# Attention and a gelu layer in parallel: dense groups on one PSUM bank of their own, with half a unit between groups

## The chip, the cores and the metric

The kernel runs on one core of a Trainium2 chip. The metric is the device time of one execution in microseconds (us). Of the kernel before, three runs gave 1554.35, 1555.06 and 1557.26 us, with a median of 1555.06 us. One further execution was profiled; its own time is 1555.34 us, of which the profile's span covers 1553.6 us.

The engines are TensorE (PE, with its weight loads as PEld), VectorE (DVE), ScalarE (ACT), GpSimd (POOL) and SyncE (SP), which issues the DMAs.

## What is computed

The input is normalized (layer norm over 512 columns), and two branches read it: attention with 32 heads of 16 columns over 2048 rows, and a two-layer net of width 1792 with gelu (tanh form). The result is the sum of the input and both branches.

```
xn = _layernorm(x, axis=-1)
return x + _A_ref(xn, A_wqkv, A_wo) + _B_ref(xn, B_w1, B_b1, B_w2, B_b2)

# _A_ref: scores = q @ k.T * (Dh ** -0.5);  p = softmax(scores);  (p @ v) @ wo
# _B_ref: h = gelu(x @ w1 + b1);  h @ w2 + b2
```

## The kernel before

**Units and halves.** Attention is cut into 32 tiles (8 groups of 4 heads, 4 blocks of 512 queries) of 16 units each, 512 units in all. A unit has two halves, and in each of them `unit` writes the same kinds of products into TensorE's queue, in this order:

- two score products for the row maximum (`s_half`, tile `pS`), two score products for the exponential (`e_half`, tile `pT`), each as four 32-column pieces;
- four weighted sums (`v_half`, tile `pV`, fp32, two passes each, so eight instructions in the trace), on 64 of the array's 128 rows;
- dense products (`dense`, tile `pD`, fp16) on the other 64 rows, four 32-column pieces each. The halves change sides: the first half of a unit has its dense products on rows 0 to 63, the second on rows 64 to 127.

VectorE takes the row maximum from `pS` (L259), ScalarE turns `pT` into `pe` with an exponential (L304). The order of instructions on every engine is the order in which the program writes them. Through a counter, the first weighted sum and the first dense product of a half wait for the last ones of the half before (`enter`, `leave`), because both sides add into the same banks.

**Dense work.** All matrix products outside attention are cut into groups (`Group`), of which one is open at a time: 24 projections for later heads (12 products for each side of the array), 56 hidden groups `hidden_group` (12 products a side), 32 sum groups `sum_group` (21 a side), and at the end the output projection. `dense` adds up to `pace` products of the open group to a half. For the projections the pace is `FAST`, four in every half; for hidden and sum groups it is `MEAN`, three in each half of one unit and four in each of the next. When both sides of a group are done, `ended` closes it, and ScalarE empties its bank: `pf` (L506) of a projection, `hh` (L1005) of a hidden group, `yt` (L1031) of a sum group. That instruction stands in ScalarE's queue ahead of the exponentials of the next half.

After `hh`, gelu goes three steps on GpSimd, then ScalarE's tanh (L972, two units after those steps have been written), then four steps on GpSimd, after which the piece counts as done for the sum groups (`ready`, `usable`).

**Banks.** PSUM has eight: three for `pS`, three for `pT`, one for `pD` and one for `pV`. `banks` takes the next of a kind in turn. `hold` (for the dense groups, L409 to L413) takes a bank out: the first group takes the one of kind D, and when it ends, that bank joins the end of T's list; the next group takes the bank at the head of T's list. So a bank goes round between scores and dense groups.

Of the kernel before, what the change touches and what calls it, by code (L numbers as in the profile page):

```python
# [19 lines left out]
D = 512  # L20
# [8 lines left out]
NG = H // 4  # L29
VW = DH + 1  # L30
LEAD = 20
FAST, MEAN, SLOW, LATE = (4, 4), (3, 4), (3, 3), (6, 6)
MEASURE = (3, 0, 1, 2)
HALF = 1300
POOL_NS = 2500
# [12 lines left out]
def layer_kernel(ctx: ExitStack, tc: tile.TileContext, x, wqkv, wo, w1, b1, w2, b2, out):  # L48
# [55 lines left out]
    def bank_tile(k, tag):  # L104
        return ps.tile([P, QB], F32, tag=f"B{k}", bufs=1, name="p" + tag)

    def banks(tag):
        k = free_banks[tag].pop(0)
        free_banks[tag].append(k)
        return bank_tile(k, tag)  # L110

    def hold(tag, other):
        k = free_banks[tag if free_banks[tag] else other].pop(0)
        return bank_tile(k, tag), k
# [39 lines left out]
    PAIRS = ((0, 0), (0, 1), (1, 0))  # L154
# [4 lines left out]
    def given(engine, ns):  # L159
        backlog[engine] += ns  # L160
# [52 lines left out]
    def later(n, fn, local=False):  # L213
        queue.append((slot[0] + n, fn, local))
# [10 lines left out]
    def pooled(*todo):  # L225
        steps.extend(todo)
# [169 lines left out]
    NU = NG * NQB * 16  # L396
# [10 lines left out]
    def dbank():  # L407
        turn[0] += 1
        if pos[0] < LEAD:  # L409
            return banks("T"), None  # L410
        if pos[0] > NU:
            return banks("S"), None
        return hold("D", "T")  # L413

    class Group:

# [122 lines left out]
        for _ in gen:  # L539
            pass  # L540

    pos, spent, cur = [0], [False], [None]
    feed, xbs, wcs = [], {}, {}

    def fetch_x(b):
        if b < NQB:
            xbs[b] = feed[0].tile([P, 2, NC, QB], F16, name="xb", bufs=1)
            for c in range(NC):
                later(1 + c, lambda c=c: nc.sync.dma_start(xbs[b][:, :, c], xn_d[:, :, c, b * QB:(b + 1) * QB]))

    def fetch_w1(n):
        if n < NQB * NF:
            wcs[n] = feed[0].tile([P, 2, NC, P], F16, name="wc", bufs=3)
            nc.sync.dma_start(wcs[n], w1_d[n % NF // 2, :, n % 2])

    def group(gen):

        if cur[0] is None and not spent[0]:
            cur[0] = next(gen, 0)
            if cur[0] == 0:  # L560
                cur[0], spent[0] = None, True
        return cur[0]

    def ended():

        if cur[0] is not None and cur[0].over():
            done, cur[0] = cur[0], None
            done.end()

    def burst(gen, n):  # L570

        while n > 0 and (f := group(gen)) is not None:
            if not f.usable():
                break
            f.product(2)
            n -= 1
            ended()

    def dense(gen, side):

        f = group(gen)
        for _ in range(0 if f is None else (f.pace if pos[0] <= NU + 1 else LATE)[pos[0] % 2]):
            if not f.usable(side):
                return
            f.product(side)
# [376 lines left out]
    def mlp():  # L962
        m2 = st2p
        w2_s = m2.tile([P, 2, NF, D], F16, name="w2_s")
        b2_b = m2.tile([P, D], F32, name="b2_b")
        done = set()

        def gelu(hh, g, b, f):
            t1 = m2.tile([P, QB], F32, name="t1", bufs=2)

            def tanh():
                nc.scalar.activation(t1, t1, AF.Tanh, scale=GELU_C * GELU_A)  # L972
                given("act", 600)
                later(1, rest, True)

            def rest():
                pooled((690, lambda: nc.gpsimd.tensor_scalar(t1, t1, 1.0, gs[:, 1:2], op0=ALU.add, op1=ALU.mult)),  # L977
                       (1280, lambda: nc.gpsimd.tensor_tensor(t1, t1, hh, op=ALU.mult)),  # L978
                       (620, lambda: nc.gpsimd.tensor_scalar(g[:, 0, f, :], t1, 1.0, 0.0, op0=ALU.mult, op1=ALU.add)),
                       (1160, lambda: nc.gpsimd.tensor_tensor(g[:, 1, f, :], t1, g[:, 0, f, :], op=ALU.subtract)),  # L980
                       (0, lambda: done.add((b, f))))

            pooled((1040, lambda: nc.gpsimd.tensor_tensor(t1, hh, hh, op=ALU.mult)),  # L983
                   (620, lambda: nc.gpsimd.tensor_scalar(t1, t1, 1.0, 1.0 / GELU_A, op0=ALU.mult, op1=ALU.add)),
                   (1280, lambda: nc.gpsimd.tensor_tensor(t1, t1, hh, op=ALU.mult)),  # L985
                   (0, lambda: later(2, tanh, True)))


        HF = NF // 2
        gts, xas = {}, {}  # L990
        for k in range(NF):
            later(3 * k + 2, lambda k=k: nc.sync.dma_start(w2_s[:, :, k], w2_d[:, :, k]))
        later(12, lambda: nc.sync.dma_start(b2_b, b2[None, :].to_broadcast([P, D])))

        def hidden_group(s, f):
            b, k = s // 2, s % 2 * HF + f
            if f == 0:
                gts[s] = m2.tile([P, 2, HF, QB], F16, name="g", bufs=2)
            g, xb, wc = gts[s], xbs[b], wcs[b * NF + k]
            later(1, lambda: fetch_w1(b * NF + k + 2))  # L1000

            def hidden(hp):
                hh = m2.tile([P, QB], F32, name="hh", bufs=3)
                scale, bias = fac1[0][:, k // 2:k // 2 + 1], b1_s[:, k:k + 1]
                nc.scalar.activation(hh, hp, AF.Identity, bias=bias, scale=scale)  # L1005
                given("act", 700)
                later(1, lambda: gelu(hh, g, s, f), True)

            return Group([lambda c=c, i=i, j=j: (wc[:, i, c, :], xb[:, j, c, :]) for c in range(NC) for i, j in PAIRS],
                         dbank, hidden, pace=MEAN)  # L1010

        def sum_group(s, q):
            b, t, g = s // 2, s // 2 * 4 + q, gts[s]
            if s % 2 == 0:
                xas[t] = m2.tile([P, D], F32, name="xa", bufs=4)
                nc.sync.dma_start(xas[t], x[t * P:(t + 1) * P, :])
                later(3, lambda: pooled((1280, lambda: nc.gpsimd.tensor_tensor(xas[t], xas[t], b2_b, op=ALU.add))), True)
            xa = xas[t]
            if q == 3 and s % 2 == 0:
                fetch_x(b + 1)  # L1020
            if s == 2 * NQB - 1 and q == 1:

                ocs[2] = feed[0].tile([P, 2, NC, QB], F16, name="xb", bufs=1)
                when((NG - 2) * NQB + 2, lambda: read_o(ocs[2], 2, True), 2)
                for k in range(3):
                    acs[8 + k] = feed[0].tile([P, D], F32, name="ac", tag="wc", bufs=3)
                    later(3 + k, lambda k=k: read_acc(acs[8 + k], 8 + k))

            def store(yp):
                yt = m2.tile([P, D], F32, name="yt", bufs=2)  # L1030
                nc.scalar.activation(yt, yp, AF.Copy, scale=gs[:, 2:3])  # L1031
                given("act", 600)
                add = lambda: nc.gpsimd.tensor_tensor(xa, xa, yt, op=ALU.add)  # L1033
                put = lambda: nc.sync.dma_start(acc_d[t * P:(t + 1) * P, :], xa)
                later(1, lambda: pooled((1280, add), (0, lambda: later(4, put, True) if s % 2 else None)), True)

            return Group([lambda f=f, i=i, j=j: (g[:, i, f, q * P:(q + 1) * P], w2_s[:, j, s % 2 * HF + f, :])
                          for f in range(HF) for i, j in PAIRS], dbank, store, lambda n: (s, n // 3) in done, pace=MEAN)

        for f in range(HF):  # L1040
            yield hidden_group(0, f)
        for s in range(1, 2 * NQB + 1):
            for q in range(4):
                yield sum_group(s - 1, q)
                if s < 2 * NQB and q < 3:
                    for f in range(*((0, 3), (3, 5), (5, 7))[q]):
                        yield hidden_group(s, f)

    def when(t, fn, n=1):

        def step():
            if t in ready and (pos[0] >= NU or pos[0] % 16 in range(4, 14)):
                fn()
            else:
                later(1, step)

        later(n, step)
# [3 lines left out]
    def read_o(oc, qb, early):  # L1061
        for c in range(NC):
            n = 64 if early and c == NC - 1 else P
            nc.sync.dma_start(oc[:n, :, c, :], ot_d[c * P:c * P + n, :, qb * QB:(qb + 1) * QB])  # L1064

    def read_acc(ac, t):
        nc.sync.dma_start(ac, acc_d[t * P:(t + 1) * P, :])
# [123 lines left out]
```

## Time and profile before

| what | value |
|---|---|
| median of three runs | 1555.06 us |
| the profiled execution: its time, its span | 1555.34 us, 1553.6 us |
| TensorE busy | 1514.5 us (97%) |
| VectorE busy | 1401.0 us (90%) |
| ScalarE busy | 1251.6 us (81%) |
| GpSimd busy | 674.6 us (43%) |
| weighted sums (`pV`) | 8192 instructions, 8 per half |
| exponentials, row maxima | 2048 each, 598 and 684 ns in the mean |
| `hh`, tanh, `yt`, `pf` | 56 of 778 ns, 56 of 631 ns, 32 of 689 ns, 21 of 599 ns |

Times inside the trace are counted from the start of the span. Starts are what to read on TensorE: instructions of different rows and columns of the array overlap, and their ends are modelled. The time from the first `pV` of a half to the first `pV` of the next is called the length of the half here. In a table by windows, the number in brackets behind a busy time is the number of instructions that start in the window, up to one at its edge; 8 of `pV` are one half, and 4 of `pD` are one dense product.

### The profile page before, as it was taken

What the parts mean: (1) busy time and instruction counts of PE and PEld (TensorE: products, weight loads), DVE (VectorE), ACT (ScalarE), POOL (GpSimd) and SP (SyncE); (2) the same over time, 40 slices, a digit from 0 to 9 for tenths busy, and PEclk for the clock granted to TensorE, in tenths of its full rate; (3) what the DMA queues carried; (4) which work ended last, traced back from release to release, by engine and by line L of the source; (5) the groups of instructions that cost most, each with busy time, mean ns of one, the idle gap of its engine ahead of it and who ended that gap; (6) DMA issues with size and microseconds to landing.
All of it is one profiled execution on the core that took longest, in us unless ns stands there. A gap on an engine that the chain in (4) does not pass through costs nothing.

```text
span 1553.6 us, 86338 instructions
## 1 busy us (share of the span) xinstructions
PE 1514.5 (97%) x39203; PEld 806.0 (52%) x39203; DVE 1401.0 (90%) x2372; ACT 1251.6 (81%) x2326; POOL 674.6 (43%) x694
## 2 busy tenths in 40 slices
PE   8998999999999999999999999999999999999997
PEld 4434545555555555555555555555555555555443
DVE  7898989999999999999999999999999999999612
ACT  4316878889888888888888888888888888888771
POOL 3113697546465444435443443555254454521000
PEclk9999999999999999999999999999999999999997
DMA  6454576542111311121112111121112111022412
GB/s 210 124 158 142 167 231 197 180 120 88 50 35 47 91 33 34 36 75 42 35 56 65 46 35 35 35 80 55 36 42 60 45 35 35 22 66 60 150 50 86
DMA packets 113671, 123.72 MB, mean 80 GB/s; under 512 B 24988, under 2 KB 85276, under 8 KB 113304
## 3 DMA queue, kind: packets, MB, share of 16 engines
q1 hardware_dynamic: 113304, 118.21, 25.4%
q8 instruction: 306, 5.01, 1.4%
q14 instruction: 61, 0.50, 0.1%
HBM read 80.61 MB, written 37.34 MB: 76 GB/s over the span
## 4 chain that ended last, share of the span: by engine, by line
PE 84%; DVE 8%; ACT 2%; issue 2%; DMA 2%; SPq 1%; POOL 0%; ACTq 0%; POOLq 0%
PE pV L169 25%; PE pS L169 19%; PE pD L169 19%; PE pT L169 17%; DVE mt L259 6%; PE pT L439 1%; PE pS L439 1%; ACT pe L304 1%; ACT t L972 1%; DVE amx L667 1%; PE pT L532 1%; PE pD L439 1%; DMA ac<-acc_d 0%; PE pV L532 0%; SPq L1064 0%
## 5 line engine op out<-in xcount | busy, mean ns | idle before, releaser
L259 DVE TENSOR_REDUCE mt<-pS 128x1 f32<-128x512 f32 x2048 | 1299.9, 684 | 60.7 <-PE pS L169 43.1
L304 ACT ACTIVATE pe<-pT 128x512 f32<-128x512 f32 x2048 | 1100.0, 598 | 169.5 <-PE pS L169 72.3
L169 PE MATMUL pV<-pe,vv 64*32 64x512 f32 x8192 | 1077.6, 595 | 0.2
L169 PE MATMUL pT<-qst,kst 64*32 64x512 f16 x8192 | 708.2, 378 | 10.4 <-ACT pe L304 8.9
L169 PE MATMUL pS<-kst,qst 62*32 62x512 f16 x8192 | 636.8, 378 | 9.3 <-DVE mt L259 6.0
L169 PEld LDWEIGHTS <-qst 62*32 62x32 f16 x8192 | 271.1, 92 | 226.8 <-issue 77.9
L169 PEld LDWEIGHTS <-kst 64*32 64x32 f16 x8192 | 270.2, 91 | 213.7 <-issue 109.5
L169 PE MATMUL pD<-xb,wc 64*32 64x512 f16 x5376 | 370.5, 377 | 0.0
L169 PE MATMUL pD<-w_s,g 64*32 64x512 f16 x5376 | 359.4, 377 | 0.0
L169 PEld LDWEIGHTS pV<-pe,vv 64*32 64x32 f32 x8192 | 181.5, 105 | 111.2 <-PE pV L169 18.0
L983 POOL TENSOR_TENSOR t<-hh 128x512 f32<-128x512 f32 x56 | 58.3, 1042 | 341.2 <-ACT hh L1005 341.2
L169 PEld LDWEIGHTS <-g 64*32 64x32 f16 x5376 | 113.8, 92 | 38.6
L169 PE MATMUL pD<-xt,wqk_h 64*32 64x512 f16 x1920 | 127.6, 377 | 3.5 <-issue 3.5
L169 PEld LDWEIGHTS <-wc 64*32 64x32 f16 x5376 | 112.6, 91 | 31.1
L360 POOL TENSOR_TENSOR osb<-osb,rb 128x512 f32<-128x512 f32 x31 | 39.9, 1287 | 128.1 <-DMA rb<-den_d 95.1
L1033 POOL TENSOR_TENSOR xa<-xa,yt 128x512 f32<-128x512 f32 x32 | 41.0, 1280 | 119.0 <-ACT yt L1031 119.0
L1070 DVE SCALAR_TENSOR_TENSOR ac<-pS,gs,ac 128x512 f32<-128x512 f32 x20 | 15.0, 751 | 67.0 <-PE pT L169 46.9
L978 POOL TENSOR_TENSOR t<-t,hh 128x512 f32<-128x512 f32 x56 | 71.8, 1283 | 4.7
L985 POOL TENSOR_TENSOR t<-t,hh 128x512 f32<-128x512 f32 x56 | 71.7, 1280 | 4.7
L980 POOL TENSOR_TENSOR g<-t,g 128x512 f16<-128x512 f32 x56 | 65.3, 1166 | 4.7
L977 POOL TENSOR_SCALAR t<-t,gs 128x512 f32<-128x512 f32 x56 | 38.8, 693 | 55.5 <-ACT t L972 55.5
L169 PE MATMUL pS<-wo_s,oc 64*32 64x512 f16 x1008 | 61.7, 378 | 0.3
(139 smaller groups left out, 881.1 us busy)
## 6 DMA issues: line engine op xcount, KB each, us to landing
wch<-in_B_w_dram SPq DMA_DIRECT2D x28, 512.0 KB
wc<-w_d SPq DMA_DIRECT2D x56, 256.0 KB
qk_d<-stg SPq DMA_DIRECT2D x32, 256.0 KB
rb<-den_d SPq DMA_DIRECT2D x124, 64.0 KB
w_d<-wsp SPq DMA_DIRECT2D x28, 256.0 KB
kst<-qk_d SPq DMA_DIRECT2D x128, 48.0 KB
qst<-qk_d SPq DMA_DIRECT2D x128, 48.0 KB
xs<-in_A_x_dram SPq DMA_DIRECT2D x16, 256.0 KB
```

Of the source, the lines that this page charges most:

```text
L169: p = nc.tensor.matmul(*args, **kw)
L259: nc.vector.reduce_max(mt_of[t][:, n, qt, kb:kb + 1], s, axis=AX.X)
L304: nc.scalar.activation(pe, st, AF.Exp, scale=exp_scale(g // 2))
L360: pooled((1280, lambda: nc.gpsimd.tensor_tensor(osb, osb, rb, op=ALU.mult)), (620, lambda: nc.gpsimd.tensor_scalar(ot[:, 0], osb, 1.0, 0.0 ...
L439: nc.tensor.matmul(self.bank, lhs, rhs, start=start, stop=self.last and self.over())
L532: nc.tensor.matmul(pj, xt[:, i, c, t * P:(t + 1) * P], wh[j][:, c, :], start=(n == 0), stop=(n == 11))
L977: pooled((690, lambda: nc.gpsimd.tensor_scalar(t1, t1, 1.0, gs[:, 1:2], op0=ALU.add, op1=ALU.mult)), (1280, lambda: nc.gpsimd.tensor_tenso ...
L978: (1280, lambda: nc.gpsimd.tensor_tensor(t1, t1, hh, op=ALU.mult)),
L980: (1160, lambda: nc.gpsimd.tensor_tensor(g[:, 1, f, :], t1, g[:, 0, f, :], op=ALU.subtract)),
L983: pooled((1040, lambda: nc.gpsimd.tensor_tensor(t1, hh, hh, op=ALU.mult)), (620, lambda: nc.gpsimd.tensor_scalar(t1, t1, 1.0, 1.0 / GELU_A ...
L985: (1280, lambda: nc.gpsimd.tensor_tensor(t1, t1, hh, op=ALU.mult)),
L1033: add = lambda: nc.gpsimd.tensor_tensor(xa, xa, yt, op=ALU.add)
```

## The change

- Dense groups take the bank of kind D, always the same one; `hold` no longer serves them, and T keeps its own three.
- When a group ends inside the main part (`LEAD <= pos <= NU`), `dense` writes nothing in the half that follows.
- Hidden and sum groups go at `FAST` too: four products a half.
- gelu's tanh is put off by one unit, once, if no group is open or the open one has at most 8 products left.

```diff
-FAST, MEAN, SLOW, LATE = (4, 4), (3, 4), (3, 3), (6, 6)
+FAST, LATE = (4, 4), (6, 6)
...
-        return hold("D", "T")
+        return banks("D"), None
...
-    pos, spent, cur = [0], [False], [None]
+    pos, spent, cur, paused = [0], [False], [None], [0]
...
             done.end()
+            paused[0] = int(LEAD <= pos[0] <= NU)
...
     def dense(gen, side):
 
+        if paused[0]:
+            paused[0] = 0
+            return
         f = group(gen)
...
-            def tanh():
+            def tanh(again=1):
+                if again and (cur[0] is None or cur[0].left(0) + cur[0].left(1) <= 8):
+                    later(1, lambda: tanh(0), True)
+                    return
                 nc.scalar.activation(t1, t1, AF.Tanh, scale=GELU_C * GELU_A)
...
-                         dbank, hidden, pace=MEAN)
+                         dbank, hidden)
...
-                          for f in range(HF) for i, j in PAIRS], dbank, store, lambda n: (s, n // 3) in done, pace=MEAN)
+                          for f in range(HF) for i, j in PAIRS], dbank, store, lambda n: (s, n // 3) in done)
```

How the change moves ScalarE's instructions shows in its queue. First the place where the first hidden groups end (`hh`, then the tanh with its tile `t`, among the exponentials `pe`; `osb` is the end of an attention tile). Before:

```order
L304 ACTIVATE pe<-pT 128x512 x14
L1005 ACTIVATE hh<-pD,b_s,fac_2410 128x512
L972 ACTIVATE t_8171<-t_8171 128x512
L304 ACTIVATE pe<-pT 128x512 x16
L1005 ACTIVATE hh<-pD,b_s,fac_2410 128x512
L972 ACTIVATE t_8536<-t_8536 128x512
```

and with the change:

```order
L304 ACTIVATE pe<-pT 128x512 x14
L1012 ACTIVATE hh<-pD,b_s,fac_2362 128x512
L304 ACTIVATE pe<-pT 128x512 x6
L979 ACTIVATE t_8730<-t_8730 128x512
L304 ACTIVATE pe<-pT 128x512 x8
L1012 ACTIVATE hh<-pD,b_s,fac_2362 128x512
```

The tanh stood right behind the next group's `hh`; now 6 exponentials (three halves) stand between them, and 8 ahead of the following `hh`. From `hh` to `hh` there were 16 exponentials, 8 halves; now there are 14, 7 halves. Over the whole queue, tanh stood directly behind `hh` 27 times and does so nowhere now; three times it stands directly behind a `yt`.

Second, a place where sum groups alternate with hidden groups. Before:

```order
L1031 ACTIVATE yt<-pD,gs 128x512
L304 ACTIVATE pe<-pT 128x512 x16
L1005 ACTIVATE hh<-pD,b_s,fac_2410 128x512
L304 ACTIVATE pe<-pT 128x512 x16
L1005 ACTIVATE hh<-pD,b_s,fac_2410 128x512
L972 ACTIVATE t_17773<-t_17773 128x512
```

and with the change:

```order
L1038 ACTIVATE yt<-pD,gs 128x512
L304 ACTIVATE pe<-pT 128x512 x14
L1012 ACTIVATE hh<-pD,b_s,fac_2362 128x512
L304 ACTIVATE pe<-pT 128x512 x10
L330 ACTIVATE osb<-pV 128x512
L304 ACTIVATE pe<-pT 128x512 x4
L1012 ACTIVATE hh<-pD,b_s,fac_2362 128x512
L304 ACTIVATE pe<-pT 128x512 x6
L979 ACTIVATE t_18021<-t_18021 128x512
```

The spacing goes from 8 halves to 7 here too, and the tanh that stood right behind the second `hh` now comes six exponentials after it.

Counted from TensorE's queue, over the 981 halves in which the row maxima are still made, the dense products per half are:

| products in the half | before | with the change |
|---|---|---|
| 4 | 439 | 791 |
| 3 | 418 | 4 |
| 2 | 112 | 1 |
| 1 | 6 | 66 |
| 0 | 6 | 119 |

The 119 halves without one come behind 56 hidden groups, 38 times behind a sum group, 21 times behind a projection and 4 times behind a group of the output projection. The 40 halves behind these 981, and the end of the program, hold the same products in both.

## The prediction

> **What bounds the kernel now.** I read the page's busy times first, then its chain of waits, then the lengths of single halves.
>
> ```profile
> PE 1514.5 (97%) x39203; PEld 806.0 (52%) x39203; DVE 1401.0 (90%) x2372; ACT 1251.6 (81%) x2326; POOL 674.6 (43%) x694
> PE 84%; DVE 8%; ACT 2%; issue 2%; DMA 2%; SPq 1%; POOL 0%; ACTq 0%; POOLq 0%
> ```
>
> TensorE carries 84% of the chain, so every term below is a length of a half on TensorE, and the other engines enter where they hold it up. Next, by windows, the `pV` instructions (eight to a half):
>
> ```profile
> 133.02:308.02 175.00, 126.90 (x952) 1.00 0.62 190
> 308.02:1425.98 1117.96, 877.86 (x6688) 1.00 0.18 51
> 1425.98:1462.21 36.23, 27.36 (x208) 1.00 0.56 173
> 264.42:271.00 6.58, 5.20 (x40) 1.00 0.44 111
> 720.94:731.31 10.37, 8.37 (x64) 1.00 0.19 56
> 739.44:741.82 2.38, 2.12 (x16) 1.00 0.05 10
> ```
>
> The first three rows are the stretch that the change touches: 952 + 6688 + 208 = 7848 instructions, 981 halves, in 1329.2 us. The others give undisturbed halves. Five in a row with four dense products each take 6.58 us: **1.316** a half. Eight inside a sum group (four with three products, four with four) take 10.37, so one with three costs (10.37 - 4 x 1.316) / 4 = **1.277**. Two with two products take 2.39 (to 741.83, a row below; the window is cut a hair short): **1.195**. The fourth product costs 0.04 us more, not a quarter of the half, because the weighted sums run beside it on the other rows.
>
> Halves without dense work, and the five behind them, are seen in the starts of `pV` (two rows to a half; the first of each counts):
>
> ```profile
> 1425.99 0.60 PE L169 MATMUL pV<-pe,vv 64*32 64x512 f32 x4
> 1427.13 0.63 PE L169 MATMUL pV<-pe,vv 64*32 64x512 f32 x4
> 1428.28 0.63 PE L169 MATMUL pV<-pe,vv 64*32 64x512 f32 x4
> 1433.65 0.60 PE L169 MATMUL pV<-pe,vv 64*32 64x512 f32 x4
> 1435.03:1436.16 1.13, 1.04 (x9) 1.00 0.91 284
> ```
>
> Two empty halves take 2.29 us, **1.14** each. The four halves from 1428.28 to 1433.65, with four products each, take 5.37 where 4 x 1.316 = 5.26 would be their price: **0.11** to get going again, since the rows on which the dense products stand still have the scores of the half before to do. The last row, by windows again, is a half with one product: **1.13** (the ninth instruction is the next half's).
>
> By these prices the 981 halves of before cost 439 x 1.316 + 418 x 1.277 + 112 x 1.195 + 12 x 1.14 = 1259.0 us. The measured 1329.2 hold 70.2 us of stalls. Where a group ends, one sees some of them (TensorE and ScalarE, in order of time; a hidden group, then a hidden group with tanh behind it, then a sum group):
>
> ```profile
> 740.68 0.63 PE L169 MATMUL pV<-pe,vv 64*32 64x512 f32 x4
> 741.83 0.63 PE L169 MATMUL pV<-pe,vv 64*32 64x512 f32 x4
> 741.91 0.78 ACT L1005 ACTIVATE hh<-pD,b_s,fac 128x512 f32<-128x512 f32 x1
> 742.59 2.05 ACT L304 ACTIVATE pe<-pT 128x512 f32<-128x512 f32 x4
> 743.22 0.40 PE L169 MATMUL pT<-qst,kst 64*32 64x512 f16 x4
> 743.44 0.61 PE L169 MATMUL pV<-pe,vv 64*32 64x512 f32 x4
> ...
> 752.27 0.63 PE L169 MATMUL pV<-pe,vv 64*32 64x512 f32 x4
> 752.41 0.78 ACT L1005 ACTIVATE hh<-pD,b_s,fac 128x512 f32<-128x512 f32 x1
> 753.09 0.62 ACT L972 ACTIVATE t<-t 128x512 f32<-128x512 f32 x1
> 754.24 0.40 PE L169 MATMUL pT<-qst,kst 64*32 64x512 f16 x4 [0.39 <-ACT pe L304]
> 754.46 0.61 PE L169 MATMUL pV<-pe,vv 64*32 64x512 f32 x4
> ...
> 730.01 0.60 PE L169 MATMUL pV<-pe,vv 64*32 64x512 f32 x4
> 731.27 0.69 ACT L1031 ACTIVATE yt<-pD,gs 128x512 f32<-128x512 f32 x1
> 731.31 0.59 PE L169 MATMUL pV<-pe,vv 64*32 64x512 f32 x2
> 732.72 0.61 PE L169 MATMUL pV<-pe,vv 64*32 64x512 f32 x4
> ```
>
> The half after the end should take 1.277. It takes 743.44 - 741.83 = 1.61 behind `hh` (0.33 too long), 754.46 - 752.27 = 2.19 behind `hh` with tanh (0.91), and 732.72 - 731.31 = 1.41 behind `yt` (0.13). The link is in the rows: `hh` stands in ScalarE's queue ahead of the half's exponentials; the first of these ends about 742.59 + 0.59 = 743.18; the score product at 743.22 wants its bank (three banks, so each waits for the exponential three places earlier); 0.22 later the weighted sums start. From the start of `hh` to that start are **1.53 us**, from `yt` 1.45.
>
> Their sum: 27 x 0.91 + 29 x 0.33 + 32 x 0.13 = 38.3 us. The projections' ends add little: six halves of a projection group with its end take 7.95 against 6 x 1.316 = 7.90, so 20 x 0.05 = 1.0.
>
> ```profile
> 297.18:305.13 7.95, 6.23 (x48) 1.00 0.77 225
> ```
>
> That leaves 70.2 - 39.3 = **30.9 us** of stalls that don't hang on group ends (tile ends, the transfers of the first 175 us, the last stage).
>
> **The change part by part.** *Pace.* 791 halves with four products: 791 x 1.316 = 1041.0. 66 with one at 1.13: 74.6. Five with two or three at 1.277: 6.4.
>
> *The empty half behind a hidden group.* The bank itself is ready: in the row of `yt`, ScalarE starts 731.27 - 730.01 = 1.26 after the start of a half with four products, so `hh` (0.78) is through at 2.04, and the empty half ends at 1.316 + 1.14 = 2.46 at the earliest. But `hh` still stands ahead of the exponentials, and T still has three banks, so the weighted sums after the empty half can't start before 1.26 + 1.53 = 2.79. The empty half takes 2.79 - 1.316 = **1.47** in place of 1.14: 56 x 1.47 = 82.3. This is the step where I expect most of the wish behind a pause to be lost. Bounds: 1.14 if I am wrong on the link, 1.95 (one exponential more, spaced (2.05 - 0.60) / 3 = 0.48) if ScalarE comes to `hh` late.
>
> *Behind a projection* the bank is emptied 0.18 faster (599 against 778 ns, table above): 2.61 - 1.316 = 1.29, times 21: 27.1. *Behind a sum group* the last two halves have one product a side; its dense work ends some 0.6 earlier, `yt` is out of the way by then, and 1.14 stands. With the other places: 42 x 1.14 = 47.9. There the restart counts, for 32 sum groups and 4 of the output projection: 36 x 0.11 = 4.0. Behind `hh` it is inside the 1.47, since the rows are long free by then.
>
> *tanh.* Its own 631 ns stay, but behind 4 to 8 exponentials rather than behind `hh`. A single one there stalls nothing that I can find in a half of 1.32, of which two exponentials take 0.96. Late next are its four steps on GpSimd (43% busy), and behind them sum groups, which read that piece a dozen halves later; without that cover, a unit of 2.6 us each time. The load of the next weights, written when a group opens, keeps two groups of lead, some 18 us; no wait for it shows before.
>
> *Sum.* 1041.0 + 74.6 + 6.4 + 82.3 + 27.1 + 47.9 + 4.0 = 1283.3, plus the 30.9 that stay = 1314.2 against 1329.2: **15 us less**. From the profiled execution's 1555.34 (0.28 above the median) this makes 1540.3; I say **1541**. So the stalls of 39.3 go, but 24.3 come back: fours are dearer than the mixture, and the 56 empty halves hold a stall of 0.33 each (18.5 us) that has only moved.
>
> VectorE doesn't become the bound: two row maxima back to back need 1.21 a half (0.61 apart, from the row below), and 1314.2 / 981 = 1.34.
>
> ```profile
> 861.54 1.29 DVE L259 TENSOR_REDUCE mt<-pS 128x1 f32<-128x512 f32 x2
> ```
>
> **The rivals.** *The empty half hides `hh` after all* (chance 0.17): if the scores run ahead in it, 56 x 0.33 = 18.5 us more are won: 1522. For it: scores need no dense bank any more. Against: the score at 743.22 waits for an exponential, not for the dense bank.
>
> *Nothing won* (0.13): fours in the long stage cost 1.335 instead of 1.316, 791 x 0.019 = 15 us: 1555. For it: in the first 175 us all halves have four and take 175.00 / 119 = 1.47, though with DMAs at 0.62 of their time against 0.18 later. Against: the run at 1.316 lies in that same stage.
>
> *Slower* (0.11): one bank is too few. TensorE takes its queue in order; if ScalarE reaches `hh` one exponential late, the next group's first product stands at the head of the queue waiting for the bank and keeps everything behind it: 0.48 x 56 = 26.9 us, 1568. It decides from 15 / 56 = 0.27 us per hidden group on. For it: ScalarE is 81% busy, and two exponentials with `hh` need 2 x 0.48 + 0.78 = 1.74 us, more than an empty half of 1.14. Against: `yt` in the rows above started 0.24 after the last dense product.
>
> The Trainium skill (Perfetto Trace Analysis, Optimizing Tensor Performance) says: "Independent matmul groups should rotate through different PSUM banks so the ACT/DVE evacuation of one overlaps the next group's matmuls". The kernel before does just that and the change gives it up; by that rule this rival is the likely outcome. In this trace the rotation has a price of its own, the stalls of 0.13 to 0.91 above, so I give the rule no more than that chance.
>
> *Not what it says* (inside the first case): three tanh still follow a `yt` directly; 3 x 0.5 is within the rounding.
>
> **How the numbers follow.** The sum has 0.59, with its own range of 1532 to 1549 (prices of fours uncertain by 0.007 make 5.5 us, the 1.47 by 0.1 makes 5.6). With the others the range is 1524 to 1555; it leaves out most of the slower case. Measured runs differ by some 0.2%, 3.1 us, so faster means below 1552. Faster: 0.59 + 0.17 = 0.76; same 0.13; slower 0.11.
>
> **What would show it.** Right: no `pT` waiting for `pe` behind a tanh; windows of 7 halves from `hh` to `hh` of about 9.4 us (1.47 + 6 x 1.316 = 9.37); `pV` starts 2.8 us after the start of a hidden group's last half; runs of fours at 1.316. Wrong: 9.0 (first rival), 9.5 and more with a first `pD` that waits for `hh` (slower), or fours above 1.33.

## The result: 1563.6 us, slower

| | median, runs | ratio to before, 95% interval |
|---|---|---|
| before | 1554.70 us, 20 | |
| with the change | 1563.57 us (1558.53 to 1567.54), 20 | 1.0056 [1.0045, 1.0067] |

The change costs 8.9 us where 14 were to be won. The profiled execution after has a span of 1562.3 us (before 1553.6).

### The profile after

Busy times and the chain of waits, from the page of the kernel after:

```profile
PE 1521.2 (97%) x39203; PEld 793.0 (51%) x39203; DVE 1403.2 (90%) x2372; ACT 1246.5 (80%) x2326; POOL 673.8 (43%) x694
PE 88%; DVE 5%; ACT 2%; DMA 2%; issue 1%; SPq 1%; POOL 0%; ACTq 0%; DVEq 0%; POOLq 0%
```

TensorE carries more of the chain (88% instead of 84%) with the same 39203 instructions. Where the time lies is seen by windows of the `pV` instructions (window, length, busy time and count, TensorE's granted clock, DMA share, GB/s). The rows are pieces of the 981 halves: numbers 151 to 164 (from 0), 165 to 950, and the last 30. Before (the whole, 1329.2 us, stands in the prediction):

```profile
351.34:370.29 18.95, 14.71 (x112) 1.00 0.29 83
370.29:1420.79 1050.50, 825.29 (x6288) 1.00 0.17 47
1420.79:1462.21 41.42, 31.54 (x240) 1.00 0.51 157
```

and after, with the whole in the first row:

```profile
131.03:1470.75 1339.72, 1032.25 (x7848) 1.00 0.24 72
349.54:374.23 24.69, 15.85 (x112) 0.93 0.39 114
374.23:1425.45 1051.22, 822.02 (x6288) 1.00 0.17 49
1425.45:1470.75 45.30, 33.10 (x240) 0.96 0.44 141
```

The stretch grew by 10.54 us. Of these, 5.74 lie in 14 halves around 360 us and 3.88 in the last 30 halves; both pieces show a lowered clock. The long middle piece, 786 halves with nearly all the group ends, grew by 0.72. So two things want an explanation: two single places that cost 9.6 us, and a middle that won nothing.

What TensorE waits for (in total, times, the longest), before:

```profile
PE pT L169 <- ACT pe L304: 8.9, 22, 0.8
PE pS L169 <- DVE mt L259: 6.0, 12, 1.4
```

and after:

```profile
PE pS L169 <- DVE mt L259: 10.5, 12, 3.1
PE pT L169 <- DMA qst<-m_d: 6.7, 2, 3.8
PE pT L169 <- ACT pe L304: 3.0, 8, 1.1
```

The waits for exponentials, which the change is about, fell by 5.9 us. A wait of 3.8 us for a DMA is new, and so is one of 3.1 us for a row maximum. (The other wait for that DMA, 2.9 us at 224 us, lies in the first 151 halves, which are no longer than before on the whole: 218.50 against 218.32 us.)

### The first place: SyncE's queue is jammed at a tile's end

At a tile's end the row maxima go out to DRAM (`m_d<-mhl`, L284) and come back as two more rows of Q (`qst<-m_d`, L289); then the next tile's scores can start. When VectorE has them ready, in the kernel after (one line's instructions in this part of the span: count, durations in ns, first and last start):

```profile
L281 DVE SCALAR_TENSOR_TENSOR mhl<-pS,mhl x1: 217/217/217, 349.5 to 349.5; 64x64 f16<-64x64 f32 x1
```

SyncE's queue and, in the last row, TensorE (start, duration, instruction):

```profile
335.71 4.92 SPq L403 DMA_DIRECT2D kst<-qk_d  x8
...
349.47 1.84 SPq L403 DMA_DIRECT2D qst<-qk_d  x4
...
351.83 2.84 SPq L403 DMA_DIRECT2D qst<-qk_d  x4
...
355.38 1.23 SPq L284 DMA_DIRECT2D m_d<-mhl  x2
...
361.36 0.43 PE L169 MATMUL pT<-qst,kst 64*32 64x512 f16 x8 [3.81 <-DMA qst<-m_d]
```

The maxima are ready at 349.5 + 0.2 = 349.7. SyncE takes them at 355.38, 5.7 us later, because it is still working through the loads of the next heads' K and Q (32 DMAs in all, some 0.6 us of the queue each, of which 24 stand ahead of the maxima here) and of weights. TensorE idles 3.81 us. Before, the same queue:

```profile
321.73 4.38 SPq L403 DMA_DIRECT2D kst<-qk_d  x8
...
343.33 1.82 SPq L403 DMA_DIRECT2D qst<-qk_d  x4
...
348.62 0.53 SPq L992 DMA_DIRECT2D w_s<-w_d  x1
351.48 1.85 SPq L284 DMA_DIRECT2D m_d<-mhl  x2
```

There all 32 loads were through at 345.15, and from 349.15 on SyncE waited for the maxima. What moved the loads are the 21 empty halves behind projections: the kernel writes these loads only once the last projection is done. The products of the projections, before and after (first and last start):

```profile
L169 PE MATMUL pD<-xt,wqk_h x1920: 372/376/388, 127.2 to 304.5; 64*32 64x512 f16 x192
```

```profile
L169 PE MATMUL pD<-xt,wqk_h x1920: 372/376/388, 127.6 to 329.9; 64*32 64x512 f16 x192
```

The last projection comes 25 us later, and the loads start 14 us later, at 335.71 instead of 321.73; the last eight of them go out only behind the maxima, from 360.95 on. The other runs bear this out: with the pause and the loads as here these 14 halves take 24.24 to 26.27 us (three runs), without the pause 18.51 to 18.82 (five versions; before, 18.95).

The idle time costs twice. TensorE by windows, behind the gap:

```profile
362.20:365.60 3.40, 3.40 (x68) 0.52 0.37 104
```

A microsecond after the restart the granted clock falls to a half for 3.4 us (0.52 in this row); by these two numbers an estimated 1.6 us of work are lost. The Trainium skill ("TensorE: Matmul & The Clock Gate", "Why this matters for your kernels") warns of gaps of more than about 3 us between bursts for this reason; the trace agrees, with a gap of 3.81 us.

### The second place: the same queue, in the last stage

SyncE, VectorE and TensorE of the kernel after (`ac` are partial results that the output projection adds to; `den_d` and `dn` are the softmax sums, which go out, come back in another shape, and are inverted on VectorE):

```profile
1440.90 5.90 SPq L1074 DMA_DIRECT2D ac<-acc_d  x9
1447.17 2.16 SPq L342 DMA_DIRECT2D den_d<-osb  x4
1449.77 2.58 SPq L1074 DMA_DIRECT2D ac<-acc_d  x4
1452.52 1.35 SPq L345 DMA_DIRECT2D dn<-den_d  x1
...
1456.59 0.34 DVE L348 RECIPROCAL dn<-dn 64x32 f32<-64x32 f32 x1 [3.43 <-DMA dn<-den_d]
...
1457.54 0.40 PE L169 MATMUL pS<-kst,qst 62*32 62x512 f16 x4 [3.07 <-DVE mt L259]
```

Nine loads of `ac` stand ahead of the sums and four more ahead of their return; before, three and three. VectorE waits 3.43 us for `dn` with the row maxima queued behind it, and TensorE 3.07 us for these. Here too the clock is halved afterwards: 0.51 from 1458.0 to 1461.4 us. That part isn't in every execution: two other runs with the same loads of `ac`, in which the gap here was 1.75 and 2.02 us, show no drop of the clock and 43.7 and 43.6 us for the last 30 halves (with the change 45.30, before 41.42).

### The middle: the stalls changed their place

Summed over the starts of `pV` in halves 165 to 950, against the prediction's prices for undisturbed halves:

| us | before | after |
|---|---|---|
| all 786 halves at undisturbed prices | 1006.0 | 1006.9 |
| over the price: halves in which `hh` or `yt` is emptied (82 before) | 31.7 | 1.4 |
| empty halves behind hidden groups (53; predicted 17.5) | | 16.8 |
| empty halves behind sum groups (36; predicted 0) | | 9.6 |
| halves right behind an empty one (85) | | 6.6 |
| other halves with four products | 9.8 | 7.3 |
| the rest | 3.0 | 2.6 |
| sum | 1050.5 | 1051.2 |

Some 30 us of stalls left the halves behind the ends, and 33 appeared in the empty halves and right behind them. A hidden group's end after (TensorE and ScalarE in order of time; the first row is the last half's first `pV`):

```profile
885.41 0.59 PE L169 MATMUL pV<-pe,vv 64*32 64x512 f32 x1
...
886.68 0.78 ACT L1012 ACTIVATE hh<-pD,b_s,fac 128x512 f32<-128x512 f32 x1
...
887.36 2.05 ACT L304 ACTIVATE pe<-pT 128x512 f32<-128x512 f32 x4
888.00 0.40 PE L169 MATMUL pT<-qst,kst 64*32 64x512 f16 x4
888.21 0.61 PE L169 MATMUL pV<-pe,vv 64*32 64x512 f32 x4
```

This went as predicted: `hh` starts 1.27 after the last half, the score at 888.00 waits for the first exponential behind `hh` (887.36 + 0.59), and 888.21 - 885.41 = 2.80 (predicted 2.79). A sum group's end did not:

```profile
830.77 0.39 PE L169 MATMUL pD<-w_s,g 64*32 64x512 f16 x4
830.91 1.09 ACT L304 ACTIVATE pe<-pT 128x512 f32<-128x512 f32 x2 [0.28 <-PE pS L169]
831.82 0.63 PE L169 MATMUL pV<-pe,vv 64*32 64x512 f32 x4
831.88 0.69 ACT L1038 ACTIVATE yt<-pD,gs 128x512 f32<-128x512 f32 x1
833.12 0.64 PE L169 MATMUL pV<-pe,vv 64*32 64x512 f32 x4
```

The one dense product of the last half is over at 831.16, but `yt` starts at 831.88: ScalarE has the half's two exponentials first. The short last half hardly brings the evacuation forward (over the 28 such ends in the middle without a tanh, `yt` starts 1.21 us after the start of the last half in the median; before, 1.26); it lets TensorE arrive earlier, and the empty half (it starts in the row at 831.82) takes 833.12 - 831.82 = 1.30 where 1.14 was predicted. Three of the 36, in which a tanh stands directly behind `yt`, take 2.00 us each and hold 2.6 of the 9.6 us.

### The profile page after: what moved, and what is told of

The parts are those of the page before. It is cut to its first block, busy times and chain, and to the rows that moved or that the text cites. A ratio compares the mean times of both kernels' runs of the same rounds, so it can differ in the third digit from the quotient of the medians.

```text
span 1562.3 us, 86348 instructions
## 1 busy us (share of the span) xinstructions
PE 1521.2 (97%) x39203; PEld 793.0 (51%) x39203; DVE 1403.2 (90%) x2372; ACT 1246.5 (80%) x2326; POOL 673.8 (43%) x694
## 4 chain that ended last, share of the span: by engine, by line
PE 88%; DVE 5%; ACT 2%; DMA 2%; issue 1%; SPq 1%; POOL 0%; ACTq 0%; DVEq 0%; POOLq 0%
PE pV L169 30%; PE pD L169 20%; PE pS L169 18%; PE pT L169 16%; DVE mt L259 3%; ACT pe L304 1%; PE pT L439 1%; PE pS L439 1%; DVE amx L671 1%; DMA ac<-acc_d 1%; DMA m_d<-mhl 1%; PE pT L532 1%; ACT hh L1012 1%; PE pD L439 1%; PE pV L532 0%
## 5 line engine op out<-in xcount | busy, mean ns | idle before, releaser
L169 PE MATMUL pT<-qst,kst 64*32 64x512 f16 x8192 | 699.4, 378 | 11.6 <-DMA qst<-m_d 6.7
L169 PE MATMUL pS<-kst,qst 62*32 62x512 f16 x8192 | 622.7, 379 | 12.0 <-DVE mt L259 10.5
L169 PEld LDWEIGHTS <-qst 62*32 62x32 f16 x8192 | 298.6, 92 | 308.3 <-issue 101.7
L169 PE MATMUL pD<-xb,wc 64*32 64x512 f16 x5376 | 352.0, 379 | 0.0
L169 PEld LDWEIGHTS <-kst 64*32 64x32 f16 x8192 | 237.1, 91 | 156.6 <-issue 77.6
L169 PEld LDWEIGHTS pV<-pe,vv 64*32 64x32 f32 x8192 | 186.6, 105 | 109.0 <-PE pV L169 13.2
```

The lines of the kernel that those rows point to most:

```text
L169: p = nc.tensor.matmul(*args, **kw)
```

## The experiments

Each ran five rounds beside the kernel before. Only the last four expectations reckon with the two jams. "Middle" is the piece of 786 halves above (before 1050.5 us), "first place" the 14 halves (before 18.95), "last 30" the end (before 41.42). Theory A says that the evacuation's place in ScalarE's queue, ahead of the exponentials, makes the stall at a group's end, however many banks the dense groups use.

### The tanh alone

The kernel before with the change's lines on tanh, and nothing else.

```diff
-            def tanh():
+            def tanh(again=1):
+                if again and (cur[0] is None or cur[0].left(0) + cur[0].left(1) <= 8):
+                    later(1, lambda: tanh(0), True)
+                    return
```

> The kernel before with one part of the change alone: tanh is put off by one unit when the open group has at most 8 products left. Theory A (a stall at a group's end comes from what stands in ScalarE's queue ahead of the next exponentials; three score banks let TensorE go on for three score products only): the 27 halves of 2.19 us behind hh with tanh become halves of 1.61 as behind hh alone, 27 x 0.58 = 15.7 us less, about 1539. Rival B (ScalarE has to do the same work at some time, so the stall only moves to the later tanh): no change, 1555.

Measured 1542.83 us, ratio 0.9933 [0.9910, 0.9956]; the stretch is 1316.96 us, 12.2 less than before. At a hidden group's end that had tanh right behind `hh`, `hh` now starts at 709.53 and the next weighted sums at 711.06: 1.53 us, the prediction's number. The predicted 0.58 for each of 27 places would be 15.7; four tanh now stand directly behind `yt` and take part of it back (a half of 2.04 each). This part alone is a clear gain, if 3 us less than theory A has. Run again beside the full ends below, with

> The same kernel as with tanh put off alone, run beside the one with full ends on the same chip, since the two were timed in different calls: Theory A says 8 us more than full ends by the stalls counted in the traces (45 halves behind hh with 16.4 us of stall against 10.9, dearer twos set against it, so rather 2 to 4 net).

it gave 1545.33 us, 0.9940 [0.9926, 0.9953].

### One bank without a pause

The run above, and the dense groups on the bank of kind D.

```diff
-        return hold("D", "T")
+        return banks("D"), None
```

> As the run with tanh put off alone, and dense groups keep their one bank; no pause, pace three and four as before. Theory A: the bank alone is a loss, since the next group's first product now waits for hh or yt, some 0.7 us after its turn, and TensorE takes its queue in order: 0.25 to 0.4 us at each of 108 group ends, 27 to 43 us more than with tanh put off alone, 1566 to 1582. Rival C (the stalls of before come from the bank going round, as the change assumes): less than with tanh put off alone, 1530 or so.

Measured 1572.84 us, 1.0112 [1.0096, 1.0128]: 30.0 us slower than with rotating banks, and 1346.92 for the stretch.

```profile
749.16 1.06 PE L169 MATMUL pV<-pe,vv 64*32 64x512 f32 x8
749.23 0.78 ACT L1008 ACTIVATE hh<-pD,b_s,fac 128x512 f32<-128x512 f32 x1
750.06 0.40 PE L169 MATMUL pD<-xb,wc 64*32 64x512 f16 x4
751.14 0.61 PE L169 MATMUL pV<-pe,vv 64*32 64x512 f32 x4
```

The next group's first product waits until `hh` is over (749.23 + 0.78 = 750.01), and TensorE keeps its order: the half takes 751.14 - 749.16 = 1.98. This is the wait that the prediction's slower rival named. The empty half does remove it.

### The pause with rotating banks

The change with its bank alone undone.

```diff
-        return banks("D"), None
+        return hold("D", "T")
```

> The changed kernel with the bank alone undone: dense groups take a bank that goes round, as before. In the empty half no dense group is open, so the scores have four banks in that time. Theory A: the score product behind hh waits for hh itself (over 2.1 us after the start of the group's last half), not for the exponential behind it (2.6), so the empty half is shorter by 0.2 to 0.3 us: 109 x 0.25 = 27 us less than the changed kernel, about 1537. Rival C (a bank of its own is what keeps the scores free): as long as the changed kernel or longer, 1563 to 1575.

Measured 1549.07 us, 0.9958 [0.9943, 0.9973]; the middle takes 1036.6 us, 14.6 less than with the change. The same group's end as above:

```profile
877.01 0.59 PE L169 MATMUL pV<-pe,vv 64*32 64x512 f32 x1
878.28 0.78 ACT L1012 ACTIVATE hh<-pD,b_s,fac 128x512 f32<-128x512 f32 x1
878.32 0.60 PE L169 MATMUL pV<-pe,vv 64*32 64x512 f32 x4
879.11 0.45 PE L169 MATMUL pT<-qst,kst 64*32 64x512 f16 x8
879.45 0.63 PE L169 MATMUL pV<-pe,vv 64*32 64x512 f32 x4
880.91 0.60 PE L169 MATMUL pV<-pe,vv 64*32 64x512 f32 x4
```

`hh` stands where it stood (1.27 after the last half), ahead of the exponentials as ever, and yet the empty half takes 1.13. Both score products start at 879.11, right behind the end of `hh` (879.06) and before any exponential behind it is over. In the pause no group holds a bank, so T's list has four, and the last of them is the one that `hh` has just emptied. With the change the bank of kind D lies idle in just this half, and the scores make do with three. So the place in the queue makes the stall where T has three banks, and a fourth one takes it away, as the expectation had it; but it promised 27 us, and the time fell by 14.5, since the half behind gets longer.

The pause itself still costs its half: 1.13 and then 1.46, together 2.59 (2.66 in the mean of the 53 hidden groups' ends in the middle), where two undisturbed halves with four products take 2.63.

### The evacuation behind the first exponential

The change with `hh`, `yt` and `pf` written behind the first exponential of the empty half.

```diff
-            done.end()
             paused[0] = int(LEAD <= pos[0] <= NU)
+            if paused[0] and pos[0] < NU:
+                held_end.append(done)
+            else:
+                done.end()
+
+    held_end = []
+
+    def empty():
+        while held_end:
+            held_end.pop().end()
...
                     e_half(e, b ^ 1)
+                empty()
```

> The changed kernel, with hh, yt and pf written one place later in ScalarE's queue: behind the first exponential of the empty half instead of ahead of it. Theory A: the score product that holds the weighted sums back waits for that exponential, which now ends 0.6 to 0.7 us earlier; the empty half and the one behind it take about 2.6 us together instead of 2.85, 0.25 x 109 = 27 us less than the changed kernel, about 1536. Theory D (rival: ScalarE simply has too much to do in a short empty half, whatever the order): as the changed kernel, 1563.

Measured 1552.49 us, 0.9989 [0.9971, 1.0006]; middle 1045.7.

```profile
877.09 0.60 PE L169 MATMUL pV<-pe,vv 64*32 64x512 f32 x4
878.23 0.63 PE L169 MATMUL pV<-pe,vv 64*32 64x512 f32 x4
878.56 0.40 PE L169 MATMUL pD<-xb,wc 64*32 64x512 f16 x4
879.85 0.61 PE L169 MATMUL pV<-pe,vv 64*32 64x512 f32 x4
```

The empty half falls to 878.23 - 877.09 = 1.14, as theory A has it, but `hh` is over later, and now the next group's first `pD` waits for the one bank: the half behind takes 879.85 - 878.23 = 1.62. So the expectation missed: together the two take 2.76, not 2.6, and the middle is 5.5 us shorter, not some 25. The rest of the 11 us by which the time fell against the change lies in the first 151 halves (210.4 us instead of 218.5) and wasn't followed up.

### The change without its tanh

```diff
-            def tanh(again=1):
-                if again and (cur[0] is None or cur[0].left(0) + cur[0].left(1) <= 8):
-                    later(1, lambda: tanh(0), True)
-                    return
+            def tanh():
```

> The changed kernel with tanh alone undone (it is issued when its turn comes). By its order, 7 halves from hh to hh already move tanh two or more exponentials away from every hh, so putting it off has little left to do here: Theory A expects 0 to 3 us more than the changed kernel, 1563 to 1566. If putting tanh off is worth 12 us here as it was in the kernel before, about 1575.

Measured 1559.61 us, 1.0029 [1.0015, 1.0043], less than either expectation; the middle takes 1052.6, 1.4 more than with the deferral. What wins 12 us in the kernel before wins next to nothing here: with 7 halves from end to end no tanh stands directly behind an `hh` anyway (none of the 56), and the deferral puts three of them directly behind a `yt` (empty halves of 2.00 us, 0.86 over the price). In the profiled executions the time without the deferral is shorter in the first 151 halves and the last 30 (216.5 and 43.7 us instead of 218.5 and 45.3), which isn't put down to the tanh.

### Full and light halves at the ends, without a pause

Both are the first run (tanh alone, rotating banks), with the pace counted from a group's start: hidden groups 4, 2, 2, 4 and sum groups 4, 3, 3, 3, 4, 4 products a half ("full ends"), or 2, 4, 4, 2 and 3, 4, 4, 4, 3, 3 ("light ends").

```diff
+            self.step = [0, 0]
...
-        for _ in range(0 if f is None else (f.pace if pos[0] <= NU + 1 else LATE)[pos[0] % 2]):
+        n = 0 if f is None else LATE[0] if pos[0] > NU + 1 else f.pace[min(f.step[side], len(f.pace) - 1)]
+        if f is not None:
+            f.step[side] += 1
+        for _ in range(n):
...
-                         dbank, hidden, pace=MEAN)
+                         dbank, hidden, pace=(4, 2, 2, 4))
```

> The kernel with tanh put off alone (banks going round, no pause), with the products of a group dealt out so that its first and last units carry four a half: hidden groups 4, 2, 2, 4 by units in place of the mixture of three and four that ends on two; sum groups 4, 3, 3, 3, 4, 4. Theory A: the weighted sums two halves behind a group's last half start can't come before 2.79 us (hh) or 2.71 us (yt) whatever the products are; two halves with four need 2.63 of it anyhow, two with two and three only 2.43, so the stall goes from 0.33 to about 0.16 behind hh and from 0.13 to 0.08 behind yt: some 10 us less than tanh put off alone, 1530 to 1536. Rival E (stalls are set by the mean amount of dense work, or by fours being dear): as tanh put off alone or longer, 1543 to 1548.

> The counterpart: hidden groups 2, 4, 4, 2 by units, sum groups 3, 4, 4, 4, 3, 3, all else as with tanh put off alone; the same counts of fours and twos in hidden groups as with full ends. Theory A: two halves with two products need 2.39, so 0.4 us of the 2.79 are stall at each hidden group, and 0.15 behind yt: 0.2 to 0.25 us x 56 more than with full ends, 1542 to 1550. Rival E: as with full ends.

Measured 1541.55 us, 0.9915 [0.9899, 0.9932], with full ends and 1548.08, 0.9954 [0.9940, 0.9969], with light ones; middle 1038.6 and 1043.1. With full ends a hidden group's last half starts at 733.36, `hh` at 734.62 and the half after the next at 736.15: 2.79 again. In the medians over the hidden groups of the middle, the evacuation starts 1.22 (tanh alone), 1.26 (full ends) and 1.22 us (light ends) after the start of the last half, and the weighted sums 1.53 after that in all three: it makes next to no difference what the halves hold, so it pays to fill them. Full and light ends are told apart by their intervals; full ends and the tanh alone aren't, and the 10 us that the expectation promised from it were 2.4 in the middle. Emptying the halves at an end, which is what a pause does, is the wrong way round as long as T has three banks.

With full ends four tanh still follow a `yt`. Put off twice where needed (`again=2`), with the full ends run again beside it:

> As with full ends, but tanh may be put off twice, so that it no longer stands directly behind a yt (4 places). Theory A: a tanh behind yt costs as one behind hh did, 0.58 us more than yt alone; 4 x 0.6 = 2.4 us less than with full ends, within what these runs can just tell apart. Nothing else should move.

> The kernel with full ends again, on the same chip as tanh put off alone and as two deferrals: 2 to 4 us less than tanh put off alone.

1540.37 us, 0.9906 [0.9891, 0.9921], and 1543.18, 0.9924 [0.9911, 0.9938]; middle 1036.7 and 1038.6. Both beat the kernel before and the change; between the two, and between them and the tanh alone beside them (1545.33), the intervals don't decide.

### The jams

First the loads of K and Q alone: one load (four DMAs) every second unit rather than every unit. In the traces 12 of these DMAs rather than 24 then stand ahead of the maxima (the expectation counts 20 and 32).

```diff
-        if g + 2 < NG and pos[0] - LEAD >= 64 * (g + 1) + 3:
+        if g + 2 < NG and pos[0] - LEAD >= 64 * (g + 1) + 3 and pos[0] % 2 == 0:
```

> The change, with the loads of the next heads' K and Q (four DMAs each, 32 in all on SyncE's queue) written one every second unit rather than one every unit, so that 20 of them rather than 32 stand ahead of the tile end's store of the row maxima; nothing else is moved. Theory Q (two jams of SyncE's queue make nearly the whole loss): the 14 halves from number 151 on, which take 24.70 us with the change and 18.95 before, go back to about 18.9, and the time from 1563.6 to about 1557.8. Theory E (the loss is spread over the ends of the groups; the wait at this place takes the place of others): the 14 halves may be shorter, but the time stays at 1562 to 1565.

Measured 1556.61 us, 1.0008 [0.9995, 1.0022]: no slowdown is left that could be told. SyncE's queue at the tile's end, and below it the `pV` of the first place by windows:

```profile
349.39 1.23 SPq L284 DMA_DIRECT2D m_d<-mhl  x2
```

```profile
349.13:368.24 19.11, 14.64 (x112) 1.00 0.38 103
```

The maxima go out at 349.39, not 355.38; the 14 halves take 19.11 us (24.69 with the change) at full clock.

Then the loads of `ac` as well, spaced so that three stand ahead of the sums and three ahead of their return.

```diff
-                    later(2 + k % 4, lambda k=k: read_acc(acs[k], k))
+                    later(2 + 3 * (k % 4), lambda k=k: read_acc(acs[k], k))
```

> As the run with the loads spread, and in the last stage the loads of the partial results (ac, 13 DMAs) are written three at a time every third unit, so that three rather than nine stand ahead of the last-but-one tile's sums and six rather than thirteen ahead of their return, as in the kernel before. Theory Q: the stretch of the last 30 halves goes from 45.3 us to about 41.4 as well, and the time to about 1554, no difference from before (1554.7); no wait for the row maxima's reload and none over 2 us for a row maximum is left. Theory E: 1560 or more.

Measured 1555.33 us, 0.9991 [0.9980, 1.0001]: no difference from before. The last 30 halves:

```profile
1424.11:1464.19 40.08, 31.38 (x240) 1.00 0.50 158
```

45.30 with the change, 43.57 with the first move alone, 40.08 now. In the time this second move can't be told from the first alone. The middle is what it was, 1051.3. So without the jams of SyncE's queue nothing is left of the loss, and the dense groups' new manner is worth nothing in the sum. Both moves weren't tried on the kernel before; the last 30 halves come out 1.3 us shorter than there, so a part of what they win may not be owed to the jams.

Last, both moves on the version with rotating banks, and with tanh put off twice where needed:

> The same two moves of DMAs on the change with rotating banks (1549.1 us; its 14 halves from 151 on take 24.24, its last 30 halves 44.53). Theory Q: 5.6 and 3.5 us less, about 1540. Theory E: 1547 to 1550.

> The run before it with tanh put off twice where needed, so that none stands directly behind yt (three places of some 0.85 us): 2.5 us less by either theory, about 1537.5 by theory Q, and then as good as or better than the best kernel so far (1540.4); 1545 to 1548 by theory E.

Measured 1538.48 us, 0.9884 [0.9866, 0.9902], and 1539.56, 0.9893 [0.9874, 0.9911]. The first has the lowest median of all; the second deferral wins 1.5 us in the middle (1037.9 to 1036.4) that can't be told in the time. Its expectation took the 0.85 us of each place from the kernel with one bank; with rotating banks the empty half with `yt` and tanh takes 1.17 and only the half behind it is long (1.91). The intervals of these two overlap with that of the full ends with two deferrals.

Taken one after the other, the parts come to the following in the stretch of 981 halves (the steps are read from single profiled executions; their first 151 halves, with the early transfers, differ by up to 2.5 us among these five for no reason found here; the third row holds the two moves of DMAs, too, which may win something of their own):

| | stretch, us | step |
|---|---|---|
| before | 1329.2 | |
| tanh put off | 1317.0 | -12.2 |
| pause and four products a half, jams removed | 1312.9 | -4.1 |
| the jams | 1321.7 | +8.8 |
| one bank | 1339.7 | +18.0 |

With the jams removed first, one bank costs 16.7 us (1329.6 against 1312.9), so the order matters little. Four products a half without a pause, and the pause at the old pace, weren't tried, so the row with both doesn't tell one from the other.

## Why the prediction was wrong

**Right.** Halves with four products in the middle have a median of 1.320 us (price 1.316). The empty half behind a hidden group, the step with the mechanism in it: 1.457 in the mean of 53, predicted 1.47. From one hidden group's empty half to the next, 31 stretches of seven halves in the middle have a median of 9.47 us, predicted 9.37. No tanh behind `hh`, and waits for exponentials down from 8.9 to 3.0 us. The stalls of 38.3 us at group ends were mostly there (31.7 us in the 82 of them that lie in the middle, where the prediction's prices give 24 x 0.91 + 27 x 0.33 + 31 x 0.13 = 34.8) and did go.

**Where the miss lies.** The stretch was to take 1314.2 us and took 1339.7, 25.5 more. The two jams hold 9.6 of these, and the empty halves behind sum groups another 9.6; the rest is several smaller terms, such as the 3.1 us of stalls that had been counted too many and 3.8 us of restart behind hidden groups. The jams made a loss of it; without them the gain was still missing, as the run with both moves shows (0.9991).

**"plus the 30.9 that stay" failed, and made the change slower.** The prediction took the tile ends and the last stage as stalls "that don't hang on group ends". They hang on them by way of SyncE's queue. It priced the 21 empty halves behind projections as lengths on TensorE (27.1 us) and did not ask what else a projection's end sets off: 32 loads, which the pauses moved 14 us on, up to a tile's end. Where the change moved the DMAs on SyncE's queue could have been seen beforehand; of the DMAs the prediction looked at the weights' loads alone. What failed measured 9.6 us (5.7 and 3.9), and with both queues in order the time was that of before.

**"yt is out of the way by then, and 1.14 stands" failed.** In the middle 36 empty halves took 1.406 in the mean, 9.6 us over the price (2.6 of it in the three with a tanh behind `yt`, which the prediction put at 3 x 0.5 and left out as rounding). The step followed TensorE (the dense work ends early) and forgot its own rule, that an evacuation stands in ScalarE's order behind the exponentials of the group's last half. Halves with one product were dear as well (1.19 in the mean instead of 1.13), and the restart struck behind hidden groups too, where the prediction had it hidden in the 1.47: 6.6 us right behind empty halves in the middle, 3.8 of them behind hidden groups, where 4.0 were predicted for the whole.

**The tanh's part came from elsewhere.** Of the 39.3 us, 27 x 0.58 = 15.7 are the tanh's, and they went as the sum has it, but not by the deferral. That wins 12.2 alone; here the 7 halves from end to end have already moved every tanh away from an `hh`, and the deferral on top wins 1.4 us of the middle. The time wasn't missed by this.

**The one bank's price was looked for in the wrong place.** The slower rival had 1568 and came nearest (1563.6), but by accident: no first `pD` waits for the bank with the change. What one bank costs, 18.0 us in the stretch, is the fourth bank that the scores would have had in the empty half. The prediction wrote "T still has three banks" and took it as given, though in the pause it is the change that makes it so. The Trainium skill's rule on rotating banks ("Perfetto Trace Analysis", "Optimizing Tensor Performance") was given that rival's chance of 0.11 and no more; the runs bear it out without a pause, where one bank costs 30.0 us. With a pause rotating banks win as well (0.9884 against 0.9991, the queues in order both times), but because the freed bank serves the scores. With rotation and the queues in order the kernel takes 1538.5 us, near the 1541 predicted, but that is another kernel.

## What to carry to other kernels

When work is put off, list everything that its end sets off, on every queue, and look at what stands there when it arrives: a tile's end that needs a round trip through DRAM is where a few loads in one queue cost TensorE 4 us, and its clock for 3.4 more. A pause on the bound engine is no cover for a step that waits its turn on another engine; give the waiting step a further buffer, or fill the time. And stalls summed over a trace don't add up as gains: two repairs of the same place, here the tanh's deferral and the spacing of 7 halves, win it once.

## What the runs showed of the hardware

- The five gaps of 3.07 to 4.06 us on TensorE in full work (two in the kernel after, one in each of three other runs with the pause) all went with 3.4 or 6.8 us at half the granted clock, which began between 1.2 us ahead of the restart and 1.0 us behind it. Of the shorter ones some did: one of 1.95 us (rotating banks with the pause) and one of 1.96 us (full ends) were followed by 3.4 us at half the clock, others of 2.02, 2.89 and 2.91 us were not. Before, and in the run with the loads spread, the first place shows 1.00.
- A half without dense work saves next to nothing together with the half behind it: with rotating banks the two make 2.59 us (1.13 and 1.46) in the place shown and 2.66 in the mean of 53, where two halves with four products make 2.63.
- A DMA whose data were ready waited 5.7 us on SyncE's queue behind other DMAs' issue, while the DMA engines' mean busy share in those 14 halves was 0.39.
